# GpSimd in the first batch: one operation per step, started behind VectorE's conversion

## The chip, the cores and the metric

The kernel runs on one core of a Trainium2 chip (trn2). The metric is the device time of one execution in microseconds (us). A core has five engines that run their own instruction streams and wait for one another by semaphores: TensorE (PE; its weight loads are listed as PEld), VectorE (DVE), ScalarE (ACT), GpSimd (POOL) and SyncE (SP), which here only issues DMAs. SBUF is the memory that all of them work in, PSUM the one that TensorE writes to.

## The reference

The reference is a pooled attention followed by a feed-forward block. Neighbouring rows of q are averaged in pairs, so that 1152 queries become 576 per head; attention goes over 4 batches of 8 heads with 1152 keys of width 64. The outputs of the 8 heads, side by side, are the rows of x (4 x 576 x 512).

```python
q_pool = q.reshape(B, H, S // 2, 2, D).mean(axis=3)
scores = scale * np.matmul(q_pool, k.transpose(0, 1, 3, 2))
attn = np.exp(scores - np.max(scores, axis=-1, keepdims=True))
attn = attn / (np.sum(attn, axis=-1, keepdims=True) + 1e-09)
x = heads_side_by_side(np.matmul(attn, v))
xn = (x - mu) / np.sqrt(var + 1e-06) * g_ln
out = x + np.maximum(xn @ w_ch1, 0.0) @ w_ch2
```

w_ch1 is 512 x 2048, w_ch2 is 2048 x 512. Everything is given and returned in fp32.

## The kernel before

The attention is cut into 144 steps (`step(i)`, L956): 16 pairs of heads p, four pairs to a batch, nine steps to a pair. Step i takes 128 query rows: VectorE reduces the scores of 128 x 1152 in PSUM to their row maxima (`emit_max`, L381), ScalarE makes the exponentials, TensorE computes the scores of step i + 1 and multiplies earlier exponentials with v. Each engine runs its instructions in the order in which the code issues them (`manual_schedule`); nothing reorders them.

In the first batch (steps 0 to 35, `on_pe`) the exponentials are transposed on TensorE in fp32 (L428), and the weights of the feed-forward block are made ready beside the attention. Later batches transpose by DMA instead, with the exponentials split into two fp16 parts, on VectorE (L418) or, in three steps of nine, on GpSimd (L257 and L416). From the middle of the second batch's first pair on, feed-forward units (L600 first layer, L632 second) stand between the steps of the attention.

The weights come in 32 loads, one in each of steps 0 to 31. What is done with each:

- *Conversion.* Four steps after the load VectorE runs three instructions on 128 x 512 integers in SBUF: a shift, then two that combine two tensors (`w_conv`; all three run through a queue and have line L109 in the trace, where the tensors are called stage and wsl). In the first batch they stand in each step behind the maximum of the step. Behind them come the low halves of the transposed k and q (L283, L306), whose other input is in PSUM.
- *Splits.* When the eight loads of one of four parts are in, the scale of the part is found, and GpSimd splits four tiles of 128 x 1024: `w_split_a` scales a tile in place (L257), `w_split_b` rounds it to fp16 (L257), `w_split_c` subtracts to get the low part (L788). I call them a, b and c; a part has four of each. `w_splits` (L843) sets the steps. Parts 0 and 1 are split in the first batch, starting in the step after their scale is known, parts 2 and 3 in the second, from step 36 and from step 46.

GpSimd does other things in the first batch: for p = 2 and 4 it adds the two rows of each query pair (`pool_q`, L172: the query sum) and copies the sum (`dup_q`, L178), and it copies v into its tile (`take_v`, L273, in two halves).

`at(i, fn)` puts a call at the end of step i, `pre(i, fn)` at its beginning. Instructions of GpSimd wait only for the data that they need, so their place in time beside VectorE's conversion is set by when those data are there.

Of the kernel before, what the change touches and what calls it, by code (L numbers as in the profile page):

```python
# [9 lines left out]
FP32 = mybir.dt.float32  # L10
# [14 lines left out]
def tile_pooled_attention_moe(  # L25
# [18 lines left out]
    nc = tc.nc  # L44
# [4 lines left out]
    C = S // 128  # L49
    HP = H // 2  # L50
# [18 lines left out]
    sm_p = ctx.enter_context(tc.tile_pool(name="sm", bufs=2))  # L69
# [97 lines left out]
    def pool_q(p, eng, halves=None):  # L167

        a = raws[p, "q"]
        for o, n in ((0, 128),) if halves is None else halves:  # L170
            x = a[o:o + n].rearrange("p h c r d -> p (h c) r d")
            eng.tensor_tensor(x[:, :, 0], x[:, :, 0], x[:, :, 1], op=ALU.add)  # L172

    def dup_q(p, eng, halves=None):
        a = raws[p, "q"]
        for o, n in ((0, 128),) if halves is None else halves:
            x = a[o:o + n].rearrange("p h c r d -> p (h c) r d")
            eng.tensor_copy(x[:, :, 1], x[:, :, 0])  # L178
# [76 lines left out]

    def scaled(dst, src, s=1.0):
        nc.gpsimd.tensor_scalar(dst, src, s, 1.0, op0=ALU.mult, op1=ALU.mult)  # L257

    def take_v(p, h):

        st = pair[p]
        vr = raws[p, "v"]
        if "v" not in st:

            st["v"] = tr_p.tile([128, 2, C, 130], FP16, tag="v", name="vt")
            if on_pe(p * C):
                st["v"] = st["v"].bitcast(FP32)
                nc.gpsimd.memset(st["v"][:, :, :, 64:65], 1.0)
            else:
                nc.gpsimd.memset(st["v"][:, :, :, 64:66], 1.0)  # L270
        vt = st["v"][:, h]
        if on_pe(p * C):
            nc.gpsimd.tensor_copy(vt[:, :, 0:D], vr[:, h])  # L273
            return
        s = st["s"][:, 2:3]
        scaled(vt[:, :, 0:D], vr[:, h], s)
        scaled(vr[:, h], vr[:, h], s)
        nc.gpsimd.tensor_tensor(vt[:, :, 66:66 + D], vr[:, h], vt[:, :, 0:D], op=ALU.subtract)
# [57 lines left out]
    def on_pe(i):  # L336

        return 0 <= i < HP * C
# [38 lines left out]
    def emit_max(i):  # L377
        st = steps[i]
        mx = sm_p.tile([128, 1], FP32, tag="mx", name="mx")
        nb = st["nb"] = sm_p.tile([128, 1], FP32, tag="nb", name="nb")  # L380
        nc.vector.tensor_reduce(mx, st["s"], axis=AX.X, op=ALU.max)  # L381
        sc = pair[i // C]["sc"]
        if on_pe(i):
            st["mx"] = mx
        else:
            nc.vector.tensor_scalar(nb, mx, sc[:, 0:1], -1.0, op0=ALU.mult, op1=ALU.mult)  # L386
# [44 lines left out]
    def emit_t_copy(i):  # L431
        st = steps[i]
        for a, b in ((0, 512), (512, S)):
            nc.scalar.copy(st["pt"][:, a:b], st["s"][:, a:b])
# [359 lines left out]
    def at(i, fn, *a):  # L794
        todo.setdefault(i, []).append((fn, a))
# [3 lines left out]
    def pre(i, fn, *a):  # L799
        early.setdefault(i, []).append((fn, a))  # L800
# [5 lines left out]
    for p in range(1, NP):  # L806
        i0 = (p - 1) * C
        at(max(i0 - 1, 0), load, p, "k", nc.sync)
        at(i0, load, p, "v", nc.sync)
        at(i0 + 1, bound, p, "k")  # L810
        if p % 2 == 0:
            at(i0 - 2, load_q, p, (nc.sync,))
            pre(i0 + 1, pool_q, p, nc.gpsimd)
            at(i0 + 1, dup_q, p, nc.gpsimd)
            at(i0 + 2, bound, p, "q")
        elif p == 1:
            upper = (64, 64)
            pre(0, behind_scales)
            pre(i0 + 1, pool_q, 1, nc.gpsimd, (upper,))
            at(i0 + 1, dup_q, 1, nc.gpsimd, (upper,))  # L820
            at(i0 + 2, bound, 1, "q", *upper)
        else:
            at(i0 + 1, same_q, p)
        if not on_pe(p * C):
            at(i0 + 2, bound, p, "v")
        pre(i0 + 3, scales_reduce, p, 0, 2 if on_pe(p * C) else 3)
        for n in range(2):
            at(i0 + (5, 7)[n], take_v, p, n)
        for n, (fn, u) in enumerate(PREPS):
            late = 1 if on_pe(i0) else 0  # L830
            pre(i0 + 4 + n + late, lambda fn=fn, p=p, u=u: preps.append((fn, p, u)))

    for m in range(32):
        i0 = m
# [5 lines left out]

    this = [0]

    def w_splits(part):  # L843
        for n in range(4):
            i0 = this[0] + 1 + 3 * n // 2 if part < 2 else 16 + 10 * part + 5 * n // 2
            for x, fn in ((0, w_split_a), (1, w_split_b), (2, w_split_c)):
                at(i0 + x, fn, 4 * part + n)

# [107 lines left out]
    def step(i):  # L956
        live = i < NSTEP
        this[0] = i
        for fn, a in early.pop(i, ()):
            fn(*a)  # L960
        if live:
            emit_max(i)
        if on_pe(i - 1):
            emit_t_copy(i - 1)
            steps.pop(i - 1)
        while found:
            found.popleft()()
        first = on_pe(i - 2) or on_pe(i)
        if first and not on_pe(i):
            a_piece(i)  # L970
        if on_pe(i):
            if i < 3:
                warm(16, bank())
            a_piece(i)
            a_prep()
            emit_exp(i)
        while scaled_out:
            scaled_out.popleft()()
        if i + 1 < NSTEP:
            emit_s(i + 1)  # L980
            pv_slot[0] = i + 1
        else:
            free_banks[:] = [6, 7, 0, 1, 3, 4]
            pv_slot[0] += 1
        while sums and i % 2 == sums[0][0] // 2:
            sums.popleft()[1]()
        if on_pe(i):
            while fill:
                drip()
            flush()  # L990
        else:
            flush()
            if live:
                emit_exp(i)
                emit_hi(i)
        if 0 <= i - 1 < NSTEP and not on_pe(i - 1):
            emit_lo(i - 1)
            steps.pop(i - 1)
            drip()
        norm(i)  # L1000
        while soon or len(fill) > 3:
            drip()
        if on_pe(i):
            emit_t(i)
            if reds:
                found.append(reds.popleft()())
        elif reds:
            evacs.append(reds.popleft()())
        while turned:
            n, ot = turned.popleft()  # L1010
            emit_turn(n, ot, i)
        if not on_pe(i):
            if not first:
                a_piece(i)
            some_units(i)
            a_prep()
        for fn, a in todo.pop(i, ()):
            fn(*a)

    def warm(n, ps=None):  # L1020
        ps = psum[:, 2, 0:128] if ps is None else ps[:, 0:128]
        for _ in range(n):
            nc.tensor.matmul(out=ps, lhsT=ident16, rhs=ident16, start=True, stop=True)

    with tc.manual_schedule():
# [50 lines left out]
        i = 0  # L1076
# [32 lines left out]
```

## Time and profile before

| What | Value |
|---|---|
| Time, median of 3 runs (lowest, highest) | 882.64 us (880.32, 884.5) |
| The profiled execution's own time | 883.46 us |
| Its span in the profile | 881.7 us |
| Mean granted clock of TensorE | 0.982 |
| Busy: PE, DVE, ACT, POOL | 823.7, 614.7, 570.7, 349.0 us |
| First batch, steps 0 to 35 | about 16 to 204 us of the span |

The profile is of one execution. Its page gives busy time by engine, a strip of 40 slices, and groups of instructions; the trace behind it can be asked for single instructions, for the waits of an engine, and for busy time by stretch. The start of each maximum (L381) marks the start of a step on VectorE, so the distance of two such starts is the length of a step.

### The profile page before, as it was taken

Reading aid. Unit: us, or ns where it says so; the run is one execution under the profiler, and the core shown is the slowest. Engines: PE = TensorE matmul, PEld = TensorE weight load, DVE = VectorE, ACT = ScalarE, POOL = GpSimd, SP = SyncE. Lnnn points to the kernel's source line nnn. Section 1 sums busy time; section 2 is a strip of 40 time slices with the busy share of each in tenths; the row PEclk is TensorE's granted clock in tenths of the full one; section 3 lists DMA queues with packets and bytes.
Section 4 is the critical chain, followed back from the end, with each engine's and each line's share of the span. In section 5 each row is a group of like instructions: output and inputs, shape, how many; then the busy total and the mean of one; then the engine's idle time right before and its main releaser. Section 6 shows DMA issues by size and latency. Waiting matters only on the chain.

```text
span 881.7 us, 21840 instructions
## 1 busy us (share of the span) xinstructions
PE 823.7 (93%) x9270; PEld 587.6 (67%) x9270; DVE 614.7 (70%) x1092; ACT 570.7 (65%) x851; POOL 349.0 (40%) x318
## 2 busy tenths in 40 slices
PE   8999899898898999898899999999999999999997
PEld 6778687686656575556666666566757576666764
DVE  4687989897777787778778777777877777532121
ACT  3988788887566686668676767676768676411110
POOL 3010634436776934364464345526343423300000
PEclk9999989899999999999999999999999999999999
DMA  6463436303589698969697969796988967600001
GB/s 187 149 207 120 129 120 183 120 1 87 105 146 181 129 173 162 201 132 181 118 222 124 196 126 215 125 179 113 196 155 158 175 113 135 121 13 13 16 10 24
DMA packets 276017, 115.97 MB, mean 132 GB/s; under 512 B 259280, under 2 KB 259280, under 8 KB 275920
## 3 DMA queue, kind: packets, MB, share of 16 engines
q1 hardware_dynamic: 275568, 113.70, 62.3%
q8 instruction: 72, 1.18, 0.5%
q10 hardware_dynamic: 352, 0.88, 0.4%
q14 instruction: 25, 0.20, 0.1%
HBM read 46.14 MB, written 4.72 MB: 58 GB/s over the span
## 4 chain that ended last, share of the span: by engine, by line
PE 51%; DVE 26%; ACT 13%; DMA 4%; issue 3%; POOL 1%; SPq 1%; ACTq 0%; POOLq 0%; DVEq 0%
PE psum L632 15%; PE psum L600 14%; DVE mx L381 7%; PE psum L464 6%; DVE hl L418 5%; PE psum L362 4%; PE psum L452 4%; ACT pe L395 3%; DVE stage L109 3%; DVE ht L614 2%; PE psum L428 2%; ACT ht L613 2%; DVE wsl L109 2%; PE psum L370 2%; DVE kt L283 1%
## 5 line engine op out<-in xcount | busy, mean ns | idle before, releaser
L381 DVE TENSOR_REDUCE mx<-psum 128x1 f32<-128x1152 f32 x144 | 194.4, 1350 | 20.6 <-ACT xb L519 7.0
L632 PE MATMUL psum<-wsl,ht 128*128 128x512 f16 x864 | 196.6, 379 | 3.9 <-DVE ht L614 3.4
L395 ACT ACTIVATE pe<-psum,nb,sc 128x1152 f32<-128x1152 f32 x144 | 188.9, 1312 | 12.0 <-DVE nb L386 10.5
L600 PEld LDWEIGHTS <-wsl 128*128 128x128 f16 x1920 | 171.9, 99 | 29.5 <-issue 9.2
L600 PE MATMUL psum<-xn,wsl 128*128 128x256 f16 x1536 | 181.7, 277 | 8.4 <-DVE xb L645 4.3
L632 PEld LDWEIGHTS <-ht 128*128 128x128 f16 x864 | 80.8, 98 | 92.3 <-issue 4.5
L409 ACT ACTIVATE hl<-pe 128x1152 f16<-128x1152 f32 x108 | 125.6, 1163 | 8.0 <-DMA pt<-hl 4.7
L362 PE MATMUL psum<-kt,qt 64*128 64x512 f16 (+1 forms) x960 | 127.4, 381 | 1.7 <-ACT pe L395 0.9
L614 DVE SCALAR_TENSOR_TENSOR ht<-psum,ht 128x512 f16<-128x512 f32 x72 | 49.8, 691 | 104.7 <-ACT ht L613 104.7
L464 PE MATMUL psum<-vt,pt 128*128 128x65 f16 (+1 forms) x3240 | 117.6, 194 | 0.0
L464 PEld LDWEIGHTS <-pt 128*128 128x128 f16 (+1 forms) x3240 | 109.5, 100 | 2.5 <-DMA pt<-hl 0.4
L418 DVE SCALAR_TENSOR_TENSOR hl<-pe,hl 128x1152 f16<-128x1152 f32 x72 | 109.3, 1518 | 0.0
L519 ACT ACTIVATE xb<-psum,r 128x64 f32<-128x64 f32 x128 | 39.7, 310 | 96.1 <-DVE r L515 89.0
L613 ACT ACTIVATE ht<-psum 128x512 f16<-128x512 f32 x72 | 42.7, 593 | 88.2 <-PE psum L600 87.9
L257 POOL TENSOR_SCALAR pe<-pe 128x1152 f32<-128x1152 f32 x36 | 42.0, 1168 | 140.1 <-ACT hl L409 135.4
L416 POOL TENSOR_TENSOR hl<-pe,hl 128x1152 f16<-128x1152 f32 x36 | 85.5, 2374 | 3.0
L452 PE MATMUL psum<-pt,vt 128*65 128x128 f32 (+1 forms) x720 | 82.1, 272 | 1.4 <-DVE qt L283 1.4
L452 PEld LDWEIGHTS psum<-pt,vt 128*65 128x65 f32 x720 | 76.1, 144 | 1.8 <-DVE qt L283 1.8
L362 PEld LDWEIGHTS <-qt 64*128 64x128 f16 (+1 forms) x960 | 39.8, 97 | 39.7 <-issue 22.3
L370 PEld LDWEIGHTS <-qt 128*128 128x128 f16 (+1 forms) x320 | 17.8, 99 | 72.5 <-issue 72.0
L370 PE MATMUL psum<-kt,qt 128*128 128x128 f16 (+1 forms) x320 | 41.4, 226 | 12.1 <-ACT xb L519 10.6
L283 DVE SCALAR_TENSOR_TENSOR qt<-psum,s,qt 128x384 f16<-128x384 f32 x48 | 29.5, 614 | 33.3 <-ACT qt L286 33.2
(116 smaller groups left out, 1003.8 us busy)
## 6 DMA issues: line engine op xcount, KB each, us to landing
stage<-in_moe_w_ch_dram SPq DMA_DIRECT2D x32, 512.0 KB, 5.1
kr<-in_k_dram SPq DMA_DIRECT2D x16, 576.0 KB, 4.5
qr<-in_q_dram SPq DMA_DIRECT2D x31, 288.0 KB, 6.2
vr<-in_v_dram SPq DMA_DIRECT2D x15, 576.0 KB, 4.7
out_dram<-xb SPq DMA_DIRECT2D x32, 128.0 KB, 2.5
pt<-hl SPq DMA_TRANSPOSE x108, 4.9
kr<-in_k_dram SPq DMA_DIRECT2D x16, 64.0 KB, 4.2
vr<-in_v_dram ACTq DMA_DIRECT2D x1, 576.0 KB, 6.7
```

The lines of the kernel that those rows point to most:

```text
L362: nc.tensor.matmul(out=sp[o:o + w, c0:c0 + 512], lhsT=qt[r:r + 64, qa, q0:q0 + w], rhs=kt[r:r + 64, ka, h], start=(a == 0), stop=(a == 2),)
L370: nc.tensor.matmul(out=sp[o:o + w, 1024:1152], lhsT=qt[:, qa, q0:q0 + w], rhs=pair[p]["k8"][:, h], start=(qa == 0), stop=(qa == 1),)
L381: nc.vector.tensor_reduce(mx, st["s"], axis=AX.X, op=ALU.max)
L395: nc.scalar.activation(out=st["pe"], in_=st["s"], func=ACTF.Exp, scale=pair[i // C]["sc"][:, 0:1], bias=st["nb"],)
L409: nc.scalar.activation(out=hl[:, 0], in_=st["pe"], func=ACTF.Copy, scale=2.0 ** 15)
L416: nc.gpsimd.tensor_tensor(hl[:, 1], st["pe"], hl[:, 0], op=ALU.subtract)
L418: nc.vector.scalar_tensor_tensor(hl[:, 1], st["pe"], 2.0 ** 15, hl[:, 0], op0=ALU.mult, op1=ALU.subtract)
L452: nc.tensor.matmul(out=ps[0:65, q0:q0 + w], lhsT=vt[:, h, c], rhs=pt[:, 128 * u + q0:128 * u + q0 + w], start=(u == 0), stop=(u == C - 1),)
L464: nc.tensor.matmul(out=dst[:, 0:n], lhsT=lhsT, rhs=rhs, start=(u == 0 and lhsT is hi and n == 65), stop=(u == C - 1 and lhsT is lo), skip_ ...
L600: nc.tensor.matmul(out=ps[:, o:o + n], lhsT=wsl[:, 8 * w + cc, wa, f * 128:f * 128 + 128], rhs=xn[:, xa * KD + cc, 0:n], start=(m == 0), s ...
L614: lambda: nc.vector.scalar_tensor_tensor(lo, pv, 0.0, hi, op0=ALU.max, op1=ALU.subtract),
L632: nc.tensor.matmul(out=ps, lhsT=hv[0][:, ha, f, t * 128:t * 128 + 128], rhs=wsl[:, 8 * w + 4 + f // 2, wa, (f % 2) * DM:(f % 2) * DM + DM] ...
```

## The change

A new helper, `gate()`, issues a one-column memset on VectorE and a one-column copy of it on GpSimd. Since the memset stands behind what VectorE already has in its queue, GpSimd's copy, and all that GpSimd has behind it, can't start before VectorE has come to that place.

In the first batch the splits of parts 0 and 1 no longer have steps of their own: they go into a queue (`calm`), from which the end of each step takes one operation, with a gate in front. The last step of the batch, and steps after it, take up to two without a gate. The query sums of pairs 2 and 4 and their copies go into the same queue ahead of the splits, at steps i0 - 1 and i0 (before: both in step i0 + 1), and the load of these queries is issued two steps earlier. Each half of v in the first batch gets a gate as well. The splits of parts 2 and 3 begin at steps 40 and 49 (before: 36 and 46).

```diff
+    def gate():
+        x = sm_p.tile([128, 2], FP32, tag="gate", name="gate", bufs=4)
+        nc.vector.memset(x[:, 0:1], 1.0)
+        nc.gpsimd.tensor_copy(x[:, 1:2], x[:, 0:1])
...
         if p % 2 == 0:
-            at(i0 - 2, load_q, p, (nc.sync,))
-            pre(i0 + 1, pool_q, p, nc.gpsimd)
-            at(i0 + 1, dup_q, p, nc.gpsimd)
+            if on_pe(i0):
+                at(i0 - 4, load_q, p, (nc.sync,))
+                at(i0 - 1, lambda p=p: calm.appendleft((lambda n: pool_q(p, nc.gpsimd), 0)))
+                at(i0, lambda p=p: calm.appendleft((lambda n: dup_q(p, nc.gpsimd), 0)))
+            else:
+                at(i0 - 2, load_q, p, (nc.sync,))
...
         for n in range(2):
+            if on_pe(p * C):
+                at(i0 + (5, 7)[n], gate)
             at(i0 + (5, 7)[n], take_v, p, n)
...
     def w_splits(part):
         for n in range(4):
-            i0 = this[0] + 1 + 3 * n // 2 if part < 2 else 16 + 10 * part + 5 * n // 2
+            if part < 2:
+                calm.extend((fn, 4 * part + n) for fn in (w_split_a, w_split_b, w_split_c))
+                continue
+            i0 = 22 + 9 * part + 5 * n // 2
...
+        if calm and i < HP * C - 1:
+            gate()
+        for _ in range(1 if i < HP * C - 1 else 2):
+            if calm:
+                fn, n = calm.popleft()
+                fn(n)
```

GpSimd's order before, from the query sum of pair 2 (L172) into the splits of part 0 (wsl; with gs it is a, without a second tensor b, on L788 c); line numbers are those of the kernel before:

```order
19 L172 TENSOR_TENSOR qr<-qr 128x18x64
20 L178 COPY qr<-qr 128x18x64
21 L268 MEMSET vt 128x18
22 L273 COPY vt<-vr 128x9x64 x2
23 L257 TENSOR_SCALAR wsl<-wsl,gs_84 128x1024
24 L257 TENSOR_SCALAR wsl<-wsl 128x1024
25 L257 TENSOR_SCALAR wsl<-wsl,gs_84 128x1024
26 L194 COPY acc<-acc 128x1
27 L788 TENSOR_TENSOR wsl<-wsl 128x1024
28 L257 TENSOR_SCALAR wsl<-wsl 128x1024
```

The same piece of GpSimd's order in the changed kernel, whose lines behind L256 are 6 higher (its gates are on L262 and L263):

```order
22 L263 COPY gate<-gate 128x1
23 L172 TENSOR_TENSOR qr<-qr 128x18x64
24 L263 COPY gate<-gate 128x1
25 L178 COPY qr<-qr 128x18x64
26 L263 COPY gate<-gate 128x1
27 L274 MEMSET vt 128x18
28 L279 COPY vt<-vr 128x9x64
29 L263 COPY gate<-gate 128x1
30 L279 COPY vt<-vr 128x9x64
31 L263 COPY gate<-gate 128x1
32 L257 TENSOR_SCALAR wsl<-wsl,gs_84 128x1024
33 L263 COPY gate<-gate 128x1
```

Every operation now stands behind a gate of its own; there are 27 gates in all.

VectorE's order in the changed kernel around steps 16 to 18 (L109 is the conversion, L289 the low half of q or k, L387 the maximum that begins a step):

```order
128 L109 SCALAR_TENSOR_TENSOR stage<-wsl,stage 128x512
129 L109 SCALAR_TENSOR_TENSOR wsl<-stage 128x512
130 L289 SCALAR_TENSOR_TENSOR qt<-psum,s,qt 128x384
131 L262 MEMSET gate 128x1 x2
132 L387 TENSOR_REDUCE mx<-psum 128x1
133 L518 RECIPROCAL r<-psum 64x2
134 L109 TENSOR_SCALAR stage<-stage 128x512
135 L109 SCALAR_TENSOR_TENSOR stage<-wsl,stage 128x512
136 L109 SCALAR_TENSOR_TENSOR wsl<-stage 128x512
137 L289 SCALAR_TENSOR_TENSOR kt<-psum,s,kt 128x512
138 L262 MEMSET gate 128x1
```

The gate is VectorE's last instruction of a step; the next maximum stands directly behind it, and the next conversion one maximum and one reciprocal later. In steps that hold a half of v and a split there are two gates.

At the end of the first batch GpSimd's order in the changed kernel, from the last gate into the second batch (wsl with wscl is a of part 1; L557 to L563 normalise rows of x):

```order
88 L263 COPY gate<-gate 128x1
89 L257 TENSOR_SCALAR wsl<-wsl 128x1024
90 L794 TENSOR_TENSOR wsl<-wsl 128x1024
91 L257 TENSOR_SCALAR wsl<-wsl,wscl 128x1024
92 L257 TENSOR_SCALAR wsl<-wsl 128x1024
93 L794 TENSOR_TENSOR wsl<-wsl 128x1024
94 L557 TENSOR_SCALAR rs<-mv 128x1
95 L560 TENSOR_SCALAR rs<-mv 128x1
96 L561 TENSOR_TENSOR rs<-rs,nhalf 128x1
97 L563 TENSOR_SCALAR xs<-xb,rs 128x512
```

Behind the last gate stand eight operations of part 1, seven of them issued in steps 35 to 38; before, the last operation of part 1 was issued in the first batch. TensorE's and ScalarE's orders are the same in both kernels.

## Rows read from the trace of the kernel before

**Rows 1.** The page's first part: busy time, share of the span, instructions.

```profile
PE 823.7 (93%) x9270; PEld 587.6 (67%) x9270; DVE 614.7 (70%) x1092; ACT 570.7 (65%) x851; POOL 349.0 (40%) x318
```

**Rows 2.** Busy time by stretch: its length, five engines, granted clock, DMA share, GB/s.

```profile
36.00:57.00 21.00, 21.00 (x222) 17.73 (x217) 17.52 (x33) 19.77 (x39) 0.00 (x0) 1.00 0.47 120
...
94.00:113.00 19.00, 15.26 (x152) 13.20 (x150) 18.69 (x23) 13.15 (x25) 17.61 (x12) 0.89 0.46 146
...
143.00:162.00 19.00, 14.97 (x145) 13.01 (x144) 18.76 (x21) 12.62 (x24) 18.53 (x12) 0.86 0.56 177
...
204.00:308.00 104.00, 92.15 (x1051) 62.04 (x1051) 78.53 (x137) 69.89 (x96) 78.41 (x61) 0.97 0.70 131
```

**Rows 3.** VectorE by time, steps 7 and 8: start, duration, instruction, idle before it.

```profile
46.57 1.36 DVE L381 TENSOR_REDUCE mx<-psum 128x1 f32<-128x1152 f32 x1
...
51.09 1.35 DVE L381 TENSOR_REDUCE mx<-psum 128x1 f32<-128x1152 f32 x1
...
55.38 0.75 DVE L283 SCALAR_TENSOR_TENSOR kt<-psum,s,kt 128x512 f16<-128x512 f32 x1 [0.93 <-ACT kt L286]
```

**Rows 4.** VectorE by time: maxima of steps 9, 10, 11, 16, 20, 25, 29; conversions.

```profile
56.05 1.35 DVE L381 TENSOR_REDUCE mx<-psum 128x1 f32<-128x1152 f32 x1
...
57.38 0.41 DVE L109 TENSOR_SCALAR stage<-stage 128x512 int32<-128x512 int32 x1
57.83 3.13 DVE L109 SCALAR_TENSOR_TENSOR stage<-wsl,stage 128x512 int32<-128x512 int32 x1
...
62.95 1.34 DVE L381 TENSOR_REDUCE mx<-psum 128x1 f32<-128x1152 f32 x1
...
67.46 1.35 DVE L381 TENSOR_REDUCE mx<-psum 128x1 f32<-128x1152 f32 x1
...
92.27 1.36 DVE L381 TENSOR_REDUCE mx<-psum 128x1 f32<-128x1152 f32 x1
...
117.65 1.35 DVE L381 TENSOR_REDUCE mx<-psum 128x1 f32<-128x1152 f32 x1
...
140.64 1.36 DVE L381 TENSOR_REDUCE mx<-psum 128x1 f32<-128x1152 f32 x1
...
143.03 0.41 DVE L109 TENSOR_SCALAR stage<-stage 128x512 int32<-128x512 int32 x1
...
166.70 1.35 DVE L381 TENSOR_REDUCE mx<-psum 128x1 f32<-128x1152 f32 x1
```

**Rows 5.** GpSimd by time: query sum and its copy, splits, a half of v.

```profile
57.76 2.64 POOL L172 TENSOR_TENSOR qr<-qr 128x1152 f32<-128x1152 f32 x1 [33.50 <-DMA qr<-in_q_dram]
60.47 1.49 POOL L178 COPY qr<-qr 128x1152 f32<-128x1152 f32 x1
...
99.16 0.18 POOL L194 COPY acc<-acc 128x1 f32<-128x1 f32 x1
99.31 2.13 POOL L788 TENSOR_TENSOR wsl<-wsl 128x1024 f16<-128x1024 f32 x1
...
106.77 1.05 POOL L257 TENSOR_SCALAR wsl<-wsl 128x1024 f16<-128x1024 f32 x1
...
124.12 0.66 POOL L273 COPY vt<-vr 128x576 f32<-128x576 f32 x1
...
204.07 1.12 POOL L257 TENSOR_SCALAR wsl<-wsl,gs 128x1024 f32<-128x1024 f32 x1
```

**Rows 6.** VectorE's small memset at the program's start, by time.

```profile
0.79 0.06 DVE L1034 MEMSET nhalf<- 128x1 f32 x1 [0.79 <-PEq L1093]
```

**Rows 7.** L418 in 204:308, grouped (count, busy, mean ns), then its min/median/max.

```profile
L418 DVE SCALAR_TENSOR_TENSOR hl<-pe,hl 128x1152 f16<-128x1152 f32 x12 | 21.3, 1773 | 0.0
...
L418 DVE SCALAR_TENSOR_TENSOR hl<-pe,hl x13: 1347/1710/3421, 210.1 to 309.9; 128x1152 f16<-128x1152 f32 x13
```

**Rows 8.** Conversion in 20:204, two of its three instructions: min/median/max in ns.

```profile
L109 DVE TENSOR_SCALAR stage<-stage x32: 396/409/2315, 35.0 to 199.4; 128x512 int32<-128x512 int32 x32
L109 DVE SCALAR_TENSOR_TENSOR stage<-wsl,stage x32: 676/694/3130, 35.5 to 200.3; 128x512 int32<-128x512 int32 x32
```

More of the change, by code (lines that the diff above doesn't have):

```diff
@@ L811, in tile_pooled_attention_moe @@
         if p % 2 == 0:
-            at(i0 - 2, load_q, p, (nc.sync,))
-            pre(i0 + 1, pool_q, p, nc.gpsimd)
-            at(i0 + 1, dup_q, p, nc.gpsimd)
+            if on_pe(i0):
[4 more added lines that the diff above has]
+                at(i0 - 2, load_q, p, (nc.sync,))
+                pre(i0 + 1, pool_q, p, nc.gpsimd)
+                at(i0 + 1, dup_q, p, nc.gpsimd)
             at(i0 + 2, bound, p, "q")
@@ L841, in tile_pooled_attention_moe @@
     this = [0]
+    calm = deque()
     def w_splits(part):
         for n in range(4):
-            i0 = this[0] + 1 + 3 * n // 2 if part < 2 else 16 + 10 * part + 5 * n // 2
+            if part < 2:
+                calm.extend((fn, 4 * part + n) for fn in (w_split_a, w_split_b, w_split_c))
+                continue
+            i0 = 22 + 9 * part + 5 * n // 2
             for x, fn in ((0, w_split_a), (1, w_split_b), (2, w_split_c)):
```

## The prediction

> **What bounds the kernel now.** I read the page's busy times first, then the busy times by stretch, then single instructions of VectorE and GpSimd by time. Over the whole span TensorE is busy 93% and GpSimd 40% [rows 1], so by the average alone GpSimd's order would not matter. The stretches say otherwise. From 36 to 57 us GpSimd does nothing and TensorE is busy in all 21.00 of 21 us; from 94 to 113 and from 143 to 162 us GpSimd is busy 17.61 and 18.53 of 19 us, TensorE falls to 15.26 and 14.97, VectorE is full (18.69 and 18.76), and the granted clock of TensorE falls from 1.00 to 0.89 and 0.86, so for part of these stretches TensorE ran at 1.2 GHz and not 2.4 [rows 2]. There VectorE bounds the kernel, and it does so with the same instructions as elsewhere. The reader is to see why in the single rows: the query sum on GpSimd runs from 57.76 to 60.40, and the conversion's second instruction on VectorE, begun at 57.83, takes 3.13 us, to 60.96 [rows 4, 5]; the same instruction's median is 0.694 us [rows 8]. So VectorE stood until GpSimd was through. The shift has 0.409 at the median and 2.315 at the most [rows 8].
>
> **The change part by part.** *What goes.* I take the length of a step from maximum to maximum and compare steps with GpSimd at work with steps of the same place in their pair without it. Step 7 takes 51.09 - 46.57 = 4.52 us, step 8 56.05 - 51.09 = 4.96 [rows 3, 4], step 10 67.46 - 62.95 = 4.51 [rows 4]. First places of a pair are disturbed in all pairs, so I give them 4.5, the row next to them. Step 9 takes 6.90, which is 2.4 too long. Steps 16 to 19 take 117.65 - 92.27 = 25.38 us against 4.52 + 4.96 + 4.5 + 4.51 = 18.49: 6.9 too long. Steps 25 to 28 take 166.70 - 140.64 = 26.06: 7.6 too long [rows 4]. Together 16.9 us; the time in which TensorE ran slower is in it. Steps 32 to 35 I leave out, since halves of v and normalisation keep GpSimd as busy there after the change as before. The other sites of the conversion are clean by its medians.
>
> *What comes back: overrun.* The gate is VectorE's last instruction of a step, so GpSimd's operation begins beside the next maximum, which reads PSUM and stands in rows beside busy GpSimd at its usual length. The start I estimate from rows: memset 0.06 [rows 6], signal 0.1 (between nothing and the small copy's own 0.18, chosen by hand), copy 0.18 [rows 5]: about 0.35 us behind the maximum's start. In steps bound by VectorE the next conversion begins 57.38 - 56.05 = 1.33 us behind the maximum's start [rows 4]. That leaves 0.98 us. An operation of GpSimd overruns it by what it takes above that [rows 5]: the query sum (2.64) by 1.66, its copy (1.49) by 0.51, a half of v with a second gate and a (0.66 + 0.18 + 1.12) by 0.98, b (1.05) by 0.07, c (2.13) by 1.15. By the changed order these fall in such steps as follows: query sum in steps 9 and 27, its copy in 10 and 28, v with a in 17 and 26, b in 18, c in 19. Sum 3.32 + 1.02 + 1.96 + 0.07 + 1.15 = 7.5 us. In the steps between, the conversion starts later, as in step 25 at 143.03 - 140.64 = 2.39 us [rows 4], and even c, done at 2.48, is nearly covered.
>
> Not all of the 7.5 lengthens a step, since VectorE has slack in a clean one. Its own work is 1.33 to the conversion, 0.41 + 0.69 + 0.69 for it [rows 8], the third instruction like the second, 0.75 for the low half [rows 3]: 3.87 against the 4.51 of step 10, slack 0.64; in step 8 it waits 0.93 for ScalarE [rows 3]. Taken off each overrun (0.93 for v with a, 0.64 for the rest) there remain 2 x 1.02 + 2 x 0.05 + 0.51 = 2.7 us. Bounds: 0 and 7.5. I take 2.7, since the slack is from rows of such steps.
>
> *The gates.* 27 memsets of 0.06 us [rows 6] are 1.6 us if none is hidden. Below is 0 (they stand where VectorE waits anyway), above 27 x 0.18 = 4.9, if each held VectorE as long as GpSimd's small copy takes [rows 5]. I take 1.6. Each memset also waits for GpSimd's copy four gates earlier; behind it stands the next maximum, and behind that ScalarE's exponentials. GpSimd would have to lag three steps for this to bite; with one operation per step it doesn't.
>
> *Moved past other work.* The load of the queries goes past two weight loads on SyncE's queue. GpSimd waited 33.50 us for it before [rows 5], and two steps earlier it is issued two weight loads sooner, while the weight loads behind it have three steps until they are read; I cost it at nothing. If the queries came late, the sum would start inside a conversion, as now, at 2.4 us per site.
>
> *Second batch.* Seven operations of part 1 (3 c, 2 a, 2 b) are issued in steps 35 to 38: 3 x 2.13 + 2 x 1.12 + 2 x 1.05 = 10.7 us of GpSimd [rows 5]. Parts 2 and 3 bring 8 x (1.12 + 1.05 + 2.13) = 34.4 us there in both kernels. What this costs VectorE is seen in the subtraction of L418: 12 times in 104 us, mean 1.773 against a minimum of 1.347, that is 5.1 us too much [rows 7]. In proportion, 10.7 us more bring 5.1 x 10.7 / 34.4 = 1.6 us. Bounds: 5.1 gained, if the later places all happen to be free, and 5.1 lost. I take 1.6 lost. TensorE's first use of part 1 (second layer, step 42) lies four steps behind its last split, the first use of part 2 (step 56) seven behind its last, of part 3 (step 60) two: I cost these waits at nothing, with GpSimd busy 78.41 of 104 us [rows 2].
>
> *Sum.* 16.9 - 2.7 - 1.6 - 1.6 = 11.0 us. The profiled execution took 883.46 us, so 872.5; the median of the runs before is 0.8 below that execution, which gives 871.7, and I say **872**.
>
> **A rule that speaks against it.** The row shows VectorE held to the end of GpSimd's operation, not slowed in proportion [rows 4, 5]. The Trainium skill, "SBUF — State Buffer", section "Who interferes with whom", says the same in general: the port pair that the two share is a lock for a whole instruction, and who issues second stands fully. By it a gated operation that is still running when the conversion comes costs all that is left of it. This makes the first rival.
>
> **The rivals.** *The lock is only moved.* All 7.5 us of overrun count, the slack being used up by what VectorE has to catch up with. For it: the overruns lie in the very steps where VectorE bounds now, and a half step lost can pull TensorE's clock down again (0.89, 0.86 [rows 2]). Against it: the 0.93 us wait in step 8. 16.9 - 7.5 - 1.6 - 1.6 = 6.2: 877.3 by the execution, **876.5** by the median.
>
> *TensorE is next.* What can be gained in the two stretches is TensorE's idle time there, 19 - 15.26 and 19 - 14.97, together 7.8 us [rows 2]; with 2.4 for step 9, 10.2. Less the three costs 4.3: 879.2, or **878.4**, which is at the edge of no change. For it: TensorE is busy 21.00 of 21 us when undisturbed. Against it: its 15.26 us hold matmuls at half the clock, which would shrink too.
>
> *Slower: the second batch pays.* Place: the subtractions of L418 in steps 36 to 58. Mechanism: with GpSimd's backlog of 10.7 us ahead of it, an operation is always running when VectorE subtracts, and each takes the 3.421 us that the worst of them shows [rows 7]. Price: 12 x (3.421 - 1.773) = 19.8 in place of 1.6. Then 16.9 - 2.7 - 1.6 - 19.8 = -7.2: 890.7, or **890**. It decides from 12.7 us on, that is once the mean of L418 goes above 2.8 us there. For it: GpSimd is busy three quarters of that stretch. Against it: the median is 1.710, so such long waits are few.
>
> **How the numbers follow.** Forecast 0.60; lock only moved 0.17; TensorE next 0.13; slower 0.07; the rest, 0.03, a gain above the forecast. The 0.5% that a measurement can tell from no change is 4.4 us, so faster is below 878.2 and slower above 887.1. Faster: 0.60 + 0.17 + 0.03 and a small share, 0.01, of the TensorE case, so 0.81; no change 0.12; slower 0.07. With all terms at their good ends the gain is 16.9 + 5.1 = 22.0 (860.7); at their bad ends 16.9 - 7.5 - 4.9 - 5.1 = -0.6 (883.2). All ends at once are unlikely: 865 to 882 leaves out the slower case and the tails.
>
> **What would show it.** Right: steps 16 to 19 take about 20 us in place of 25.4, steps 25 to 28 about 20 in place of 26.1; the conversion's longest second instruction stays below about 2.4 us (a query sum's overrun on top of 0.694); the granted clock in these steps is above 0.95; the first batch ends some 12 us earlier. Overruns should stand in steps 9, 19 and 27. Wrong: maxima as far apart as before with the wait moved to the first instruction of the conversion (the lock moved); TensorE without gaps in steps that are no shorter (TensorE next); the first batch shorter but L418's mean up by a microsecond in the second (slower). A memset of a gate that waits for GpSimd would be a cost that I have at nothing.

## The result: 870.3 us, and the profile after

| | before | changed kernel |
|---|---|---|
| Time, median (lowest to highest, runs) | 883.32 us (880.32 to 884.5, 4) | 870.34 us (868.64 to 871.3, 4) |
| Ratio, with 95% interval | | 0.9856 (0.9826 to 0.9886) |
| Profiled execution, its span | 883.46, 881.7 us | 870.55, 868.7 us |
| Mean granted clock | 0.982 | 0.995 |

The changed kernel was timed three more times beside later experiments; the ratios were 0.9889, 0.9886 and 0.9878. So the gain is 9.5 to 13 us; 872 was forecast, with a range of 865 to 882.

The page's first part answers to [rows 1]. GpSimd is as busy as it was; VectorE is busy 13 us less with 27 instructions more, since an instruction that is held counts as busy:

```profile
PE 814.0 (94%) x9270; PEld 580.1 (67%) x9270; DVE 601.7 (69%) x1119; ACT 569.7 (66%) x851; POOL 348.9 (40%) x345
```

Busy time by stretch, with the columns and at the times of [rows 2] (in the last two the changed kernel is some steps further on):

```profile
36.00:57.00 21.00, 21.00 (x221) 17.81 (x218) 17.52 (x36) 19.73 (x38) 2.48 (x7) 1.00 0.39 107
94.00:113.00 19.00, 18.38 (x182) 15.21 (x178) 16.25 (x30) 17.67 (x34) 7.07 (x11) 1.00 0.54 177
143.00:162.00 19.00, 16.88 (x166) 13.81 (x165) 14.69 (x33) 17.22 (x33) 7.08 (x7) 1.00 0.56 189
```

In the two stretches that were slow the granted clock is 1.00 (0.89 and 0.86 before), GpSimd is busy 7 us and not 18, and VectorE 16.25 and 14.69 us in place of 18.69 and 18.76.

VectorE by time, steps 9 and 10, 16, 19, 20, 25 and 29; it answers to [rows 4] (L387 is the maximum, before L381):

```profile
55.99 1.35 DVE L387 TENSOR_REDUCE mx<-psum 128x1 f32<-128x1152 f32 x1
56.01 0.06 DVE L262 MEMSET gate<- 128x1 f32 x1
57.33 1.91 DVE L109 TENSOR_SCALAR stage<-stage 128x512 int32<-128x512 int32 x1
...
61.15 1.35 DVE L387 TENSOR_REDUCE mx<-psum 128x1 f32<-128x1152 f32 x1
...
90.27 1.36 DVE L387 TENSOR_REDUCE mx<-psum 128x1 f32<-128x1152 f32 x1
...
104.80 1.35 DVE L387 TENSOR_REDUCE mx<-psum 128x1 f32<-128x1152 f32 x1
...
106.15 1.38 DVE L109 TENSOR_SCALAR stage<-stage 128x512 int32<-128x512 int32 x1
...
109.44 1.35 DVE L387 TENSOR_REDUCE mx<-psum 128x1 f32<-128x1152 f32 x1
...
132.44 1.36 DVE L387 TENSOR_REDUCE mx<-psum 128x1 f32<-128x1152 f32 x1
...
152.37 1.35 DVE L387 TENSOR_REDUCE mx<-psum 128x1 f32<-128x1152 f32 x1
```

GpSimd by time, the same steps; it answers to [rows 5]:

```profile
56.15 0.19 POOL L263 COPY gate<-gate 128x1 f32<-128x1 f32 x1 [4.17 <-DVE gate L262]
56.33 2.63 POOL L172 TENSOR_TENSOR qr<-qr 128x1152 f32<-128x1152 f32 x1
...
104.97 0.18 POOL L263 COPY gate<-gate 128x1 f32<-128x1 f32 x1 [3.33 <-DVE gate L262]
105.11 2.13 POOL L794 TENSOR_TENSOR wsl<-wsl 128x1024 f16<-128x1024 f32 x1
```

The gate does what it says: the query sum begins 56.33 - 55.99 = 0.34 us behind the maximum (0.35 was estimated), and the maximum beside it takes its usual 1.35. The sum ends at 58.96, 1.63 us behind the conversion's start at 57.33, and the shift is held until then: 1.91 us in place of 0.41. So an overrun is still there, but 1.50 us of holding stand where, in the same step of the kernel before, 3.13 - 0.69 = 2.44 stood [rows 4], and another 1.51 - 0.69 = 0.82 in the conversion's third instruction beside the copy of the sum.

All lengths of steps, from maximum to maximum, in us. In the first batch they repeat within 0.1 us between executions of one kernel, so they tell more than whole times, which scatter by 3 to 6 us. "Shortest" is the least sum that any kernel of this study has shown for the stretch.

| Steps | before | changed | shortest |
|---|---|---|---|
| 0 to 8 | 40.00 | 40.01 | 39.99 |
| 9 | 6.90 | 5.16 | 4.51 |
| 10 to 15 | 29.32 | 29.12 | 29.06 |
| 16 to 19 | 25.38 | 19.17 | 18.97 |
| 20 to 24 | 22.99 | 23.00 | 22.99 |
| 25 to 28 | 26.06 | 19.93 | 19.35 |
| 29 to 31 | 14.09 | 14.77 | 14.06 |
| 32 to 35 | 23.03 | 23.86 | 22.29 |
| first batch together | 187.77 | 175.02 | |
| 36 to 59 | 126.72 | 126.44 | |

In this execution the whole gain is in the first batch: 12.75 us.

### The profile page after: what moved, and what is told of

The parts are those of the page before. It is cut to its first block, busy times and chain, and to the rows that moved or that the text cites. A ratio compares the mean times of both kernels' runs of the same rounds, so it can differ in the third digit from the quotient of the medians.

```text
span 868.7 us, 21895 instructions
## 1 busy us (share of the span) xinstructions
PE 814.0 (94%) x9270; PEld 580.1 (67%) x9270; DVE 601.7 (69%) x1119; ACT 569.7 (66%) x851; POOL 348.9 (40%) x345
## 4 chain that ended last, share of the span: by engine, by line
PE 50%; DVE 24%; ACT 14%; DMA 4%; issue 4%; POOL 2%; SPq 2%; ACTq 0%; POOLq 0%; DVEq 0%
PE psum L638 15%; PE psum L606 14%; DVE mx L387 7%; PE psum L470 5%; DVE hl L424 5%; PE psum L368 4%; ACT pe L401 4%; PE psum L458 3%; DVE ht L620 2%; ACT ht L619 2%; DMA qr<-in_q_dram 2%; PE psum L434 2%; DMA vr<-in_v_dram 2%; DVE kt L289 2%; PE psum L376 1%
## 5 line engine op out<-in xcount | busy, mean ns | idle before, releaser
L387 DVE TENSOR_REDUCE mx<-psum 128x1 f32<-128x1152 f32 x144 | 194.7, 1352 | 19.5 <-ACT xb L525 6.9
L606 PE MATMUL psum<-xn,wsl 128*128 128x256 f16 x1536 | 178.7, 275 | 8.5 <-DVE xb L651 5.3
L424 DVE SCALAR_TENSOR_TENSOR hl<-pe,hl 128x1152 f16<-128x1152 f32 x72 | 113.2, 1573 | 0.0
L257 POOL TENSOR_SCALAR pe<-pe 128x1152 f32<-128x1152 f32 x36 | 43.1, 1196 | 132.4 <-ACT hl L415 132.4
L458 PE MATMUL psum<-pt,vt 128*65 128x128 f32 (+1 forms) x720 | 77.5, 263 | 2.2 <-DVE qt L289 2.2
L458 PEld LDWEIGHTS psum<-pt,vt 128*65 128x65 f32 x720 | 71.5, 138 | 2.6 <-DVE qt L289 2.6
L289 DVE SCALAR_TENSOR_TENSOR qt<-psum,s,qt 128x384 f16<-128x384 f32 x48 | 29.5, 615 | 32.6 <-ACT qt L292 32.6
L263 POOL COPY gate<-gate 128x1 f32<-128x1 f32 x27 | 5.2, 191 | 116.8 <-DVE gate L262 116.8
```

The source lines that it names most:

```text
L424: nc.vector.scalar_tensor_tensor(hl[:, 1], st["pe"], 2.0 ** 15, hl[:, 0], op0=ALU.mult, op1=ALU.subtract)
L458: nc.tensor.matmul(out=ps[0:65, q0:q0 + w], lhsT=vt[:, h, c], rhs=pt[:, 128 * u + q0:128 * u + q0 + w], start=(u == 0), stop=(u == C - 1),)
L606: nc.tensor.matmul(out=ps[:, o:o + n], lhsT=wsl[:, 8 * w + cc, wa, f * 128:f * 128 + 128], rhs=xn[:, xa * KD + cc, 0:n], start=(m == 0), s ...
```

## The experiments

Theory: GpSimd's operation holds the conversion wherever it overlaps it, but not the instructions of VectorE that read PSUM; the gate moves it beside the maximum, which does, and only what outlasts the room of a step costs. Rivals: spreading the operations is enough, without any gate; or the later places of parts 2 and 3 make the gain.

**The gates left out.** All else is as changed: one operation per step, no gate.

```diff
     def gate():
-        x = sm_p.tile([128, 2], FP32, tag="gate", name="gate", bufs=4)
-        nc.vector.memset(x[:, 0:1], 1.0)
-        nc.gpsimd.tensor_copy(x[:, 1:2], x[:, 0:1])
+        return
```

> The changed kernel without any gate: the order on every engine and the spreading over steps stay, the 27 memsets and copies go. Theory (GpSimd's operations hold VectorE's conversion, and the gates keep them apart): without a gate GpSimd runs ahead as soon as data are there, the splits bunch up beside the conversion as before, steps 16 to 19 take 24 to 26 us again and the time is 879 to 884 us. Rival (spreading the splits over steps and moving half of part 1 past the first batch does it, gates or not): 869 to 873 us.

Measured: 882.66 us, ratio 1.0012 (0.9995 to 1.0029). Nothing is left of the gain. Steps 16 to 19 take 21.02 us, not the 24 to 26 expected; what is lost stands a little later, with 28.69 us in steps 20 to 24 in place of 23.00. GpSimd by time:

```profile
97.49 1.27 POOL L257 TENSOR_SCALAR wsl<-wsl,gs 128x1024 f32<-128x1024 f32 x1 [22.86 <-DVE r L516]
98.85 1.36 POOL L257 TENSOR_SCALAR wsl<-wsl 128x1024 f16<-128x1024 f32 x1
100.29 2.44 POOL L792 TENSOR_TENSOR wsl<-wsl 128x1024 f16<-128x1024 f32 x1
```

Without gates the operations run in a row as soon as their data are there, whatever step issued them. Order in the code doesn't spread them; something to wait for does.

**The gate ahead of the conversion.** Gate and operation of each step are issued at its beginning and no longer at the end of the step before, so that the memset falls behind the maximum. The gates of v stay.

```diff
@@ step(i), ahead of the conversion
+            if calm:
+                gate()
+                fn, n = calm.popleft()
+                fn(n)
```

> The changed kernel with the gates of the splits and query sums moved from behind a step's conversion to directly in front of the next step's conversion: as many gates, one operation per step as well, some 1.5 us later. Theory (place beside the conversion decides): 21 operations of 1.05 to 2.64 us, 31 us in all, now run into the second instruction of the conversion; less 0.64 us of slack for each, about 18 us in place of the 2 us that the changed kernel loses in overruns, so 882 to 890 us. Rival (one operation per step is enough wherever it stands): 869 to 873 us.

Measured: 881.1 us, ratio 0.9989 (0.9968 to 1.001). VectorE, then GpSimd, by time:

```profile
105.65 0.42 DVE L109 TENSOR_SCALAR stage<-stage 128x512 int32<-128x512 int32 x1
105.67 0.06 DVE L262 MEMSET gate<- 128x1 f32 x1
106.11 2.66 DVE L109 SCALAR_TENSOR_TENSOR stage<-wsl,stage 128x512 int32<-128x512 int32 x1
```

```profile
106.08 2.14 POOL L794 TENSOR_TENSOR wsl<-wsl 128x1024 f16<-128x1024 f32 x1
```

Operation c begins 0.03 us ahead of the second instruction, which then lasts until 0.55 us behind c's end, in place of 0.69 us. The same gate behind the maximum and not ahead of it is worth nothing: its place decides, not its presence. The loss is smaller than expected, though: the first batch is 184.49 us, 9.5 longer than in the changed kernel, where some 16 were expected, and the whole lies just under the expected 882 to 890.

**The query sum as before**, the splits with gates:

```diff
-            if on_pe(i0):
-                at(i0 - 4, load_q, p, (nc.sync,))
-                at(i0 - 1, lambda p=p: calm.appendleft((lambda n: pool_q(p, nc.gpsimd), 0)))
-                at(i0, lambda p=p: calm.appendleft((lambda n: dup_q(p, nc.gpsimd), 0)))
-            else:
+            at(i0 - 2, load_q, p, (nc.sync,))
+            pre(i0 + 1, pool_q, p, nc.gpsimd)
+            at(i0 + 1, dup_q, p, nc.gpsimd)
```

> The changed kernel with the query sums, their copies and the load of the queries put back as before; splits and v stay gated. Theory (each operation beside the conversion costs by itself): the sum of pair 2 runs into the conversion of step 9 again, where the changed kernel has 5.16 us in place of 6.90, and pair 4's sum into a conversion of steps 26 to 28; 1.5 to 3.5 us more than the changed kernel, 872 to 874 us. Rival (only the splits matter): 869.5 to 871.5 us with step 9 as in the changed kernel.

Measured: 876.66 us, ratio 0.9938 (0.9913 to 0.9963), more than the 872 to 874 expected. VectorE by time in step 9:

```profile
57.19 1.35 DVE L387 TENSOR_REDUCE mx<-psum 128x1 f32<-128x1152 f32 x1
...
58.97 3.01 DVE L109 SCALAR_TENSOR_TENSOR stage<-wsl,stage 128x512 int32<-128x512 int32 x1
62.02 1.51 DVE L109 SCALAR_TENSOR_TENSOR wsl<-stage 128x512 int32<-128x512 int32 x1
...
63.98 1.34 DVE L387 TENSOR_REDUCE mx<-psum 128x1 f32<-128x1152 f32 x1
```

Step 9 takes 6.79 us again, steps 25 to 28 23.11 (19.93 changed), the first batch 180.76: 5.7 longer. The loss of the second sum is larger than expected since it now runs behind c in step 28 (7.79 us in place of 4.53). So the two query sums make 5.7 of the 12.75 us, and 7.0 are left for the splits and v.

**The later places of parts 2 and 3 alone**, all else as before:

```diff
-            i0 = this[0] + 1 + 3 * n // 2 if part < 2 else 16 + 10 * part + 5 * n // 2
+            i0 = this[0] + 1 + 3 * n // 2 if part < 2 else (16 + 10 * part if part < 2 else 22 + 9 * part) + 5 * n // 2
```

> The kernel before with one line of the change: parts 2 and 3 are split from steps 40 and 49 in place of 36 and 46. First batch as before. My sum gave the second batch a loss of 1.6 us for more work of GpSimd beside L418; here that work is the same and only later, so 881 to 885 us, within 0.3% of before. Rival (the second batch gains by the later start, which would hide a loss elsewhere in the changed kernel): 877 to 880 us.

Measured: 882.68 us, ratio 1.002 (0.9996 to 1.0044). They give nothing. One place shows a cost of theirs: steps 52 and 53 together take 11.89 us, and 10.88 in the profile of the kernel before, all at a granted clock of 1.00.

**Four memsets per gate**, to size the price of one, all on the element of the gate:

```diff
-        nc.vector.memset(x[:, 0:1], 1.0)
+        for _ in range(4):
+            nc.vector.memset(x[:, 0:1], 1.0)
```

> The changed kernel with four memsets in each gate in place of one, the copy as it is: 81 more memsets on VectorE. By my sum's price of 0.06 us a memset, none hidden: 4.9 us more than the changed kernel, 874 to 876 us. Theory after the trace (the memset of a gate runs beside the maximum that follows and costs VectorE next to nothing, 0.02 us): 0 to 2 us more.

Measured: 877.18 us, ratio 0.9945 (0.9923 to 0.9967); the changed kernel beside it 872.84. The first batch is 180.96 us, 5.9 longer, near the 81 x 0.06 = 4.9 of the prediction's price. But VectorE's rows show something else:

```profile
45.20 0.33 DVE L263 MEMSET gate<- 128x1 f32 x3
45.56 1.35 DVE L388 TENSOR_REDUCE mx<-psum 128x1 f32<-128x1152 f32 x1
45.59 0.06 DVE L263 MEMSET gate<- 128x1 f32 x1
```

Writing one element, each waits for the one before, and three of them take 0.33 us: this priced a chain of waits.

**The same with an element for each**, in tiles of their own:

```diff
+        for _ in range(3):
+            y = sm_p.tile([128, 1], FP32, tag="more", name="more", bufs=9)
+            nc.vector.memset(y, 1.0)
```

> Each gate of the changed kernel is followed by three more memsets of one column, each on an element of its own, so that none has to wait for another. By the prediction's price each memset costs VectorE its 0.06 us: 27 x 3 x 0.06 = 4.9 us more than the changed kernel, all of it in the first batch. Theory (a gate is nearly free because the memset lies beside the maximum that begins 0.02 us from it): 0 to 2 us more, clean steps as long as in the changed kernel (step 20 to 24 together 23.0 us).

Measured: 870.32 us, ratio 0.9866 (0.9834 to 0.9897); the changed kernel beside it 872.18 (0.9855 to 0.9917). VectorE by time:

```profile
61.64 0.06 DVE L262 MEMSET gate<- 128x1 f32 x1
61.64 1.35 DVE L390 TENSOR_REDUCE mx<-psum 128x1 f32<-128x1152 f32 x1
61.65 0.07 DVE L266 MEMSET more<- 128x1 f32 x3
62.91 0.16 DVE L521 RECIPROCAL r<-psum 128x1 f32<-128x1 f32 x1
```

Four memsets lie within 0.1 us beside the maximum's first moments. The first batch takes 175.14 us in place of 175.02: 81 memsets cost 0.12 us. The first of the two experiments had agreed with the prediction's price for a wrong reason.

**Long operations moved to longer steps.** The query sums begin in steps 6 and 24, three steps earlier, where half of v stands too; the second half of v comes one step sooner; c is kept from the last place of a pair and the first two; nothing is split from step 32 on.

```diff
-                at(i0 - 1, lambda p=p: calm.appendleft((lambda n: pool_q(p, nc.gpsimd), 0)))
-                at(i0, lambda p=p: calm.appendleft((lambda n: dup_q(p, nc.gpsimd), 0)))
+                at(i0 - 4, lambda p=p: calm.appendleft((lambda n: pool_q(p, nc.gpsimd), "q")))
+                at(i0 - 3, lambda p=p: calm.appendleft((lambda n: dup_q(p, nc.gpsimd), "q")))
...
+        elif calm and i < 32:
+            short = (i + 1) % C in (8, 0, 1)
+            if short and calm[0][0] is w_split_c:
+                x = [x for x in calm if x[0] is w_split_a][:1]
```

> The changed kernel with the long operations (query sums, c) put into steps whose conversion starts late: query sums in the sixth step of a pair in place of the first, no c ahead of a step of the last, first or second place, the second half of v one step earlier, and no split taken from step 32 on in the first batch, where normalisation and v fill GpSimd. Theory (what the changed kernel still loses is overrun: 0.66 in step 9, 0.96 in step 27, 0.6 in 17, 19 and 26, 0.7 in step 34): 1.5 to 3 us less than the changed kernel, 867 to 869 us. Rival (TensorE bounds these steps now, and a shorter VectorE gives nothing): the same as the changed kernel within 0.5 us.

Measured: 874.0 us, ratio 0.9909 (0.9879 to 0.9939), beside 872.84; 867 to 869 were expected. Step 9 falls to 4.51, steps 32 to 35 to 22.29; but step 6, where v and the query sum stand together, goes from 4.40 to 6.22 and step 24 from 4.63 to 6.15. The overrun is moved, not removed: two operations whose gates open at the same place are one long one.

**The query sum alone in its step** (steps 5 and 23), the halves of v in the changed kernel's places again, no split beside the second half. These lines are the difference from the experiment before this one:

```diff
-                at(i0 - 4, lambda p=p: calm.appendleft((lambda n: pool_q(p, nc.gpsimd), "q")))
+                at(i0 - 5, lambda p=p: calm.appendleft((lambda n: pool_q(p, nc.gpsimd), "q")))
...
-        elif calm and i < 32:
+        elif calm and i < 32 and i % C != 7:
```

> The changed kernel still loses about 1.3 us in steps 9, 17, 19 and 26, where a long operation of GpSimd is begun ahead of the last place of a pair or of the first two, and 0.8 us in steps 32 to 35. Here the query sum stands in the fifth step of a pair, alone, no c in the last place or the first two, and nothing in steps 32 to 34. Theory (what an operation overruns of the step's room is what it costs): step 9 about 4.5 us in place of 5.16, steps 16 to 19 about 18.8 in place of 19.2, steps 25 to 28 about 19.5 in place of 19.9, steps 32 to 35 about 22.3 in place of 23.9; the first batch 172 to 173 us in place of 175.0, the whole 867 to 870 beside 870 to 873 of the changed kernel on the same chip. Rival (what the first batch gives, the second takes, since more splits are left for it): the first batch shorter as said, but steps 36 to 60 longer by 2 us or more, and the whole equal to the changed kernel.

Measured: 873.34 us, ratio 0.9895 (0.9864 to 0.9927), beside 872.18; 867 to 870 were expected. The first batch is 174.41 us, not 172 to 173. Steps 9 and 32 to 35 are as short as expected, but step 5 takes 5.91 in place of 5.39, step 23 5.85 in place of 5.39, and step 24, where c now stands behind v, 5.63 in place of 4.63. VectorE by time in step 5 of this kernel (L238 to L244 work out the scales of a pair):

```profile
39.49 0.16 DVE L238 TENSOR_SCALAR red<-psum 128x2 f32<-128x2 f32 x1 [0.79 <-ACT pt L440]
39.68 0.72 DVE L243 TENSOR_SCALAR e<-red 128x2 int32<-128x2 int32 x1
```

GpSimd by time, in the same kernel:

```profile
37.77 2.62 POOL L172 TENSOR_TENSOR qr<-qr 128x1152 f32<-128x1152 f32 x1
```

The sum ends at 40.39. L243 has two columns, takes 0.17 us else, and is held until 40.40; L238, as small, reads PSUM and passes. Instructions of one column pass, though they read SBUF: in step 25 of the changed kernel c runs from 132.62 to 134.75, and beside it

```profile
134.24 0.15 DVE L764 TENSOR_SCALAR wexp<-wmax 128x1 int32<-128x1 int32 x1
```

takes its usual time. A long step only helps if its wider VectorE work of SBUF comes late in it.

**The pieces that helped.** Query sum as in the changed kernel; splits as in the last experiment, and c not beside v at all. This line is the difference from the last experiment in the splits:

```diff
-            short = (i + 1) % C in (8, 0, 1)
+            short = (i + 1) % C in (8, 0, 1, 6)
```

> The best of the pieces so far: the query sum where the changed kernel has it (ahead of the last place of a pair), no split beside the second half of v, never c beside the first half of v nor ahead of the last place of a pair and of the first two, and none in steps 32 to 34. Theory (only an operation that outlasts the room of its step costs): steps 0 to 9 40.0 us, step 9 5.16 as in the changed kernel, steps 16 to 19 18.8 in place of 19.2, steps 20 to 24 together 23.0, steps 25 to 28 19.6 in place of 19.9, steps 32 to 35 22.3 in place of 23.9; the first batch 172.7 to 173.2 us in place of 175.0, the whole 1 to 3 us below the changed kernel on the same chip, if the second batch keeps its length (126 to 130 us for steps 36 to 60). Rival: the splits left over lengthen the second batch by 2 us or more, and the whole is equal.

Measured: 868.77 us, ratio 0.9845 (0.982 to 0.987), beside 871.26 of the changed kernel (0.985 to 0.9907). The first batch is 173.54 us, 1.5 below the changed kernel's, all of it from steps 34 and 35; steps 16 to 19 take 19.06 and steps 25 to 28 19.93, where 18.8 and 19.6 were expected: steps 17 and 26 stay at 5.16 and 5.26 without a beside v, so what I had called overrun in step 17 isn't the work of a: beside v alone, too, VectorE waits for ScalarE there. It is the fastest version, though the intervals of the two overlap; the 1.5 us rest on the lengths of the steps. Step 34 in the changed kernel, VectorE and then GpSimd by time:

```profile
178.03 1.36 DVE L387 TENSOR_REDUCE mx<-psum 128x1 f32<-128x1152 f32 x1
...
179.50 2.31 DVE L109 TENSOR_SCALAR stage<-stage 128x512 int32<-128x512 int32 x1
...
182.57 1.41 DVE L109 SCALAR_TENSOR_TENSOR wsl<-stage 128x512 int32<-128x512 int32 x1
```

```profile
176.91 1.06 POOL L257 TENSOR_SCALAR vr<-vr,s 128x576 f32<-128x576 f32 x1
178.06 1.25 POOL L284 TENSOR_TENSOR vt<-vr,vt 128x576 f16<-128x576 f32 x1
179.26 0.17 POOL L263 COPY gate<-gate 128x1 f32<-128x1 f32 x1
179.39 2.12 POOL L794 TENSOR_TENSOR wsl<-wsl 128x1024 f16<-128x1024 f32 x1
...
181.82 1.63 POOL L257 TENSOR_SCALAR wsl<-wsl,wscl 128x1024 f32<-128x1024 f32 x1
```

The same step in the kernel before, VectorE and GpSimd:

```profile
193.04 2.31 DVE L109 TENSOR_SCALAR stage<-stage 128x512 int32<-128x512 int32 x1
```

```profile
192.94 2.13 POOL L788 TENSOR_TENSOR wsl<-wsl 128x1024 f16<-128x1024 f32 x1
```

And step 34 of the last kernel, VectorE:

```profile
179.39 0.43 DVE L109 TENSOR_SCALAR stage<-stage 128x512 int32<-128x512 int32 x1
```

A gate holds GpSimd back, but can't call it. The gate of c opened at 173.44, beside the maximum of step 33; GpSimd was at normalisation and then at v (to L284), so its copy comes 5.82 us later, behind the maximum of step 34, and c begins just ahead of the conversion. The gate of a, step 34's own operation, had opened at 177.94, so a follows c at once and holds the conversion's third instruction as well. The step takes 7.23 us, and 5.33 without the splits. Before, it took 6.50: c stood at the same place there and held the shift for as long, but no a came behind it.

**The changed kernel again**, beside these experiments, for the scatter.

> The changed kernel once more, beside the next two on the same chip, as the measure for them: 868 to 872 us, a ratio to before of 0.983 to 0.989.

> The changed kernel once more, beside the other two on the same chip: about 870 to 873 us, steps 0 to 36 within 0.1 us of 175.0, and steps 36 to 60 anywhere between 126.4 and 128.9.

> The changed kernel once more, beside the other one: 870 to 873 us, the first batch within 0.1 us of 175.0.

Measured: 872.84 us (867.93 to 874.13), 872.18 (871.34 to 873.4) and 871.26 (869.47 to 875.54). The first batch took 175.00, 175.04 and 175.05 us; steps 36 to 59 took 128.86, 129.80 and 132.43, against 126.44 in the profile above. TensorE by time in step 37, first in the profile above, then in the fourth one:

```profile
195.25 0.66 PE L569 MATMUL psum<-ident,xs 128*128 128x128 f32 x4
196.84 2.18 PE L458 MATMUL psum<-pt,vt 128*65 128x128 f32 x18 [0.94 <-DVE qt L289]
```

```profile
195.22 0.66 PE L569 MATMUL psum<-ident,xs 128*128 128x128 f32 x4
196.81 3.72 PE L458 MATMUL psum<-pt,vt 128*65 128x128 f32 x18 [0.94 <-DVE qt L289]
```

The same program, after the same wait of 0.94 us, runs the same 18 matmuls in 2.18 or in 3.72 us. The mean granted clock from that step 36 to step 40 is 1.00 in the one and 0.91 in the other, so part of the latter ran at 1.2 GHz. This is one of the places where the executions of one kernel part: these steps take 18.34 us in the first profile and 19.89 to 20.01 in the other three. Step 49 (7.17 us at a granted clock of 0.72 in the fourth profile, 5.61 at 1.00 in the first) is another.

## Why the prediction was right, by its own steps

**What goes (16.9 us).** Right in its mechanism, 2.1 us too large. Against the shortest lengths, step 9 was 2.39 too long, steps 16 to 19 6.41, steps 25 to 28 6.71, less 0.70 that step 29 gives back (it was short before only because its maximum came late): 14.8. Besides step 29 the error is in the lengths that I took for undisturbed: step 27, a first place of a pair, was given 4.5 us and takes 5.33 where no query sum stands in it, and steps 16 and 17 take 0.45 more than steps 7 and 8. Step 18, the other first place, does take 4.52. The gain in TensorE's clock was rightly left inside this term: by steps, 0.87 in steps 16 to 19 and in 25 to 28 became 1.00.

**Overrun (2.7 us; 7.5 before slack).** Measured 0.65 in step 9, 0.20 in steps 16 to 19, 0.58 in steps 25 to 28: 1.4. The overruns themselves were as worked out (1.63 us of the query sum against 1.66), but a step has 0.85 us of slack or more, not 0.64: in step 9 the shift is held 1.91 - 0.41 = 1.50 us and the step is 0.65 longer, in step 19 it is held 1.38 - 0.41 = 0.97 and the step is 0.12 longer; both leave 0.85; in step 27 the shift is held 1.50 us too and the step is only 0.13 longer. Some 0.5 of the 1.4 us isn't overrun: steps 16 and 17, 25 and 26 are as long in the kernel of "The pieces that helped", where no split stands beside the second half of v and VectorE waits for ScalarE (0.47 us in step 26), so about 0.9 is left. The rival that all 7.5 us count is out.

On the holding itself the Trainium skill, "SBUF — State Buffer", section "Who interferes with whom", says that an instruction of VectorE with at most one input from SBUF and outside the faster two-port forms doesn't meet GpSimd at all, and that a reduction never does. This case agrees: the maxima beside GpSimd's sum keep 1.35 us, and L238 with its input in PSUM takes 0.16 while L243 behind it is held. Its rule that the one who issued first keeps the ports for the whole instruction is what the second experiment shows, with 2.66 us for 0.69.

**Gates (1.6 us).** Nothing: 81 more memsets cost 0.12 us, so 27 cost 0.04. The row gave 0.06 us for one by itself; beside the maximum, which begins at the same moment, it takes no time of the queue. This is the lower bound of the range that was given.

**Steps 32 to 35 (left out).** This is the step of the prediction that failed. I took GpSimd to be as busy there in both kernels and put the term at nothing; the steps became 0.83 us longer, and 1.57 longer than the shortest. Step 34 makes 0.73 of it: with c beside the shift, as before, a now follows at once and holds the conversion's third instruction 1.41 - 0.69 = 0.72 us. The prediction had looked for harm from a GpSimd that lags only in a memset that waits for a copy four gates earlier, and put that at a lag of three steps; a lag of one step did harm another way, since the next gate was open by then.

The first batch by these measured terms: 14.8 - 1.4 - 0.8 = 12.6, and 0.2 from steps 10 to 15: 12.8, as against 12.75 measured and 16.9 - 2.7 - 1.6 = 12.6 predicted. The errors of 2.1, 1.3, 1.6 and 0.8 us nearly cancel: that the total came out right is luck, and it is better than its terms.

**Second batch (1.6 us lost, bounds 5.1 either way).** Over the four profiled executions steps 36 to 59 take 129.4 us on the mean, 2.7 more than in the one profile of the kernel before; 126.4 to 132.4 is their scatter. What stands behind step 60 and ahead of step 0 is 0.6 shorter on that mean, and the span 10.7 shorter, where the sum gave 11.0. The subtraction (L424, before L418), 190 to 320 us, before and after:

```profile
L418 DVE SCALAR_TENSOR_TENSOR hl<-pe,hl 128x1152 f16<-128x1152 f32 x14 | 24.4, 1745 | 0.0
```

```profile
L424 DVE SCALAR_TENSOR_TENSOR hl<-pe,hl 128x1152 f16<-128x1152 f32 x16 | 31.1, 1943 | 0.0
```

It is held some 0.2 us longer each time (0.17 to 0.33 in the other three), far from the microsecond from which the slower rival decides (by the prediction's terms from 16.9 - 2.7 - 1.6 = 12.6 us on, not 12.7). That 126.44 us are as few as the 126.72 before doesn't show that this cost nothing: the granted clock over steps 36 to 59 was 1.00 there and 0.97 before. Two other profiles of the changed kernel, at 0.97 as well though with the falls at other steps, have 128.86 and 129.80. And steps 52 and 53, at a clock of 1.00 in all five profiles, take 10.88 us before and 11.88 or 11.89 in the changed kernel; with the later places of parts 2 and 3 alone they take 11.89 too. So about 1 us of loss is shown and belongs to these later places, for which the prediction had no term of cost. Whether the rest of the 2.7 us belongs to the change or to the scatter of the one profile before stays open; the medians (9.5 to 13 us of gain against 12.75 in the first batch) lean to a small loss.

**TensorE next.** Its price is out. Steps 16 to 19, before and after, with the columns of [rows 2]:

```profile
92.27:117.65 25.38, 21.64 (x204) 18.67 (x202) 23.31 (x29) 17.73 (x34) 17.67 (x12) 0.87 0.41 133
```

```profile
90.27:109.44 19.17, 19.17 (x209) 16.23 (x208) 16.75 (x34) 17.36 (x33) 5.79 (x9) 1.00 0.54 175
```

Its idle time was 25.38 - 21.64 = 3.74 us, but the steps became 6.21 shorter, since its busy time fell too, at the higher clock, as the prediction's own argument against this rival said. What the rival says of the order is borne out: TensorE is now busy all through these steps.

## What to carry to other kernels

An engine that waits only for data may run its backlog at the worst moment; a one-column instruction on the engine that is to be spared, and a copy of it, put the work beside an instruction that it can't disturb, at next to no cost. Put the gate ahead of the instruction that reads PSUM, one operation behind each gate, and compare the operation's end with the next instruction of two or more columns that reads SBUF, however small that is. Since a gate only sets the earliest start, put nothing behind it where the gated engine may still be at something else: a late operation meets the next one, whose gate is open by then.

## What was not expected of the hardware

- Writes of VectorE to one element follow each other at 0.33 / 3 = 0.11 us, while four to elements of their own lie within 0.1 us beside a reduction.
- The same 18 matmuls behind the same 0.94 us wait took 2.18 or 3.72 us in two executions of one program, at a mean granted clock of 1.00 and 0.91, while the first batch, at a clock of 1.00, repeated within 0.05 us (175.00 to 175.05).
- An instruction of two columns is held as fully as one of 512 (0.72 us in place of 0.17), while one of a single column passes (0.15 us beside c).
